# A second level of seven block products inside the gate/up stage of a two-layer kernel on one core

## The chip, the cores and the metric

The kernel runs on one core of a Trainium2 chip. The metric is the device time of one execution in microseconds (us), taken as the median of several executions. Ratios are the mean time of one kernel's runs over the mean of the kernel before's runs in the same rounds, so they are not quite the ratio of the medians quoted beside them.

Engine names as in the profile: PE is TensorE's matmuls, PEld its weight loads, DVE is VectorE, ACT is ScalarE, POOL is GpSimd, SP the engine that issues all DMA transfers here.

## The reference

Two layers, each a linear-attention block and a gated block, with 2048 tokens of width 1024 and an inner width of 3584:

```python
def _B_ref(x, w_gate, w_up, w_down):
    g = jnp.einsum("bsd,df->bsf", x, w_gate)
    u = jnp.einsum("bsd,df->bsf", x, w_up)
    h = g * u
    return jnp.einsum("bsf,fd->bsd", h, w_down)

x = A_x
x = x + _A_ref(_layernorm(x, axis=-1), A_wqkv, A_wo)
x = x + _B_ref(_layernorm(x, axis=-1), B_w_gate, B_w_up, B_w_down)
x = x + _A_ref(_layernorm(x, axis=-1), A_wqkv, A_wo)      # same weights again
x = x + _B_ref(_layernorm(x, axis=-1), B_w_gate, B_w_up, B_w_down)
```

Only the gated block B matters here: the gate and up products, and `h = g * u`.

## The kernel before

Block B handles 1024 tokens in a *pass*; there are two gate/up passes a layer, each followed by a down pass. I call the four gate/up passes 1a, 1b (layer one) and 2a, 2b (layer two).

Gate and up are already computed with Winograd's form of Strassen's scheme: the weight block and the token block are cut 2 x 2, and seven block products (numbered 1 to 7) replace eight. A *unit* is one such block multiplication for gate or for up. Each of its products is four matmuls with 512 columns:

```python
def pe(q, bank, start):
    w, rw, x, rx = xs[q]
    P.add("pe", lambda e: [e.matmul(psb(bank), w[:, k, :], x[:, k, :], start=(start and k == 0), stop=(k == 3),
                                    skip_group_check=True) for k in range(4)], rd=rw + rx, pwr=[bank])
```

The results that several products share are copied by ScalarE out of PSUM, the memory that matmuls write to, and added on VectorE while it evicts (moves a finished result out of PSUM, times the scale `SG`). VectorE also multiplies gate by up:

```python
def fin(b, bank, ti):          # b: which of four destination tiles
    ...
    elif m == 0:               # gate
        stt(g4[b], psb(bank), SG, tm[ti][0], tm[ti][1], gr, prd=[bank])
    else:                      # up: add, then multiply with gate
        ut, ur = utmp[b % 2], R(O_UT[b % 2], 1024)
        stt(ut, psb(bank), SG, tm[ti][0], tm[ti][1], ur, prd=[bank])
        tt(hv[:, j, :], ut, g4[b], ALU.mult, ur + gr, hr)
```

The sums of weight blocks for the first level are made on VectorE in pass 1a (`prep_s`), stored to DRAM and loaded in the other passes. In pass 1a VectorE also makes the sums for w_down and stores them from a tile `dout`:

```python
def wd_store(j):
    dma(tscr[:, :, j, :].rearrange("q p c -> p q c"), dout, R(V_D + j * 32, 32), KDW, rd=R(O_DOUT, 4096))
```

All tiles lie at hand-chosen byte offsets in one on-chip area, and every `P.add` lists the bytes it reads and writes; waits follow from these bytes. The relevant offsets of the kernel before:

```python
O_DOUT = RB + 28672                                  # 4096 bytes, to RB + 32768
O_UT = [RE + 4096 + i * 1024 for i in range(2)]      # utmp, two scratch tiles
```

Every transfer is issued by SP, in program order: weights come through a ring of five slots, one unit each, with `ring_issue()`.

## Time and profile before

1497.84 us median (1497.33 to 1498.81, 6 runs). From the page of the profile, the span, the busy time of each engine, and the chain of waits, which is the work that ended last, followed back:

```profile
span 1495.1 us, 17704 instructions
PE 1479.0 (99%) x6925; PEld 660.1 (44%) x6990; DVE 913.9 (61%) x1530; ACT 449.2 (30%) x732; POOL 216.0 (14%) x239
...
PE 91%; DVE 3%; DMA 3%; issue 1%; POOL 1%; ACT 1%; SPq 0%; ACTq 0%
```

The same busy times for the four gate/up passes alone, in the table of stretches. Columns: start and end in us, length, then busy us (and instructions) of PE, PEld, DVE, ACT and POOL, the granted clock, the DMA engines' busy share, GB/s. The lines are 1a, 1b, 2a, 2b.

```profile
243.15:412.86 169.71, 168.29 (x777) 72.12 (x777) 127.53 (x285) 66.11 (x113) 2.33 (x6) 1.00 0.83 254
498.98:666.68 167.70, 167.65 (x777) 72.19 (x777) 81.70 (x140) 65.53 (x112) 6.31 (x16) 1.00 0.73 210
983.68:1152.13 168.45, 167.83 (x777) 72.17 (x777) 72.74 (x122) 67.15 (x114) 2.36 (x6) 1.00 0.57 173
1238.25:1405.95 167.70, 167.65 (x778) 72.19 (x777) 67.08 (x108) 65.53 (x112) 0.00 (x0) 1.00 0.57 180
```

PE is busy for the whole of every pass. In the chain, in order of time (start, length, what), pass 1b is one piece:

```profile
499.14 167.49 PE ps L912 x776
```

So 776 matmuls in 167.49 us, 215.8 ns each, with nothing else in the way. Fewer or shorter matmuls save time here, for as long as the other engines and the transfers keep up. Note how much room they have: VectorE uses 40 to 49% of the last three passes, but 75% of pass 1a.

### The profile page before, as it was taken

The numbers are of one execution on the slowest core, as the hardware profiler recorded it, in microseconds if no ns is written. First come the engines' busy times: TensorE is split into PE (matmuls) and PEld (weight loads), VectorE is DVE, ScalarE is ACT, GpSimd is POOL, SyncE is SP. The second block draws the span as 40 slices with busy tenths as digits, with TensorE's granted clock in tenths as the row PEclk, the third lists the DMA queues.
The fourth block names the chain that finished last, engine by engine and source line by source line (L and its number), as shares of the span: only waits on it lengthen the run. The fifth ranks groups of instructions, "written<-read, shape, count | busy, mean of one in ns | idle before, by whom it ended". The sixth has DMA issues, their size and how long they took to land.

```text
span 1495.1 us, 17704 instructions
## 1 busy us (share of the span) xinstructions
PE 1479.0 (99%) x6925; PEld 660.1 (44%) x6990; DVE 913.9 (61%) x1530; ACT 449.2 (30%) x732; POOL 216.0 (14%) x239
## 2 busy tenths in 40 slices
PE   8999999999999999999999999999999999999999
PEld 4444444444444444444444444444444444444444
DVE  7986978777656463445488678764344553434453
ACT  3332355333300234330023314543333003334200
POOL 4544621000000010000044345310000000000000
PEclk9999999999999999999999999999999999999999
DMA  6134656799854896544466247555554455555352
GB/s 225 36 92 111 149 132 150 229 285 278 262 203 151 260 257 193 176 164 148 141 184 178 80 93 186 146 139 172 178 173 163 163 190 186 177 175 177 131 172 99
DMA packets 300643, 254.40 MB, mean 170 GB/s; under 512 B 102288, under 2 KB 266384, under 8 KB 300560
## 3 DMA queue, kind: packets, MB, share of 16 engines
q1 hardware_dynamic: 300560, 253.27, 57.4%
q8 instruction: 55, 0.90, 0.3%
q14 instruction: 28, 0.23, 0.0%
HBM read 195.04 MB, written 34.60 MB: 154 GB/s over the span
## 4 chain that ended last, share of the span: by engine, by line
PE 91%; DVE 3%; DMA 3%; issue 1%; POOL 1%; ACT 1%; SPq 0%; ACTq 0%
PE ps L912 43%; PE ps L1035 23%; PE ps L672 15%; PE ps L754 7%; PE ps L840 2%; DMA arena<-in_B_w_down_dram 1%; DVE arena L610 1%; DVE arena L412 1%; DMA arena<-arena 1%; DMA arena<-in_A_wqkv_dram 1%; POOL arena L701 1%; PE ps L766 0%; PE ps L794 0%; SPq L386 0%; POOL arena L417 0%
## 5 line engine op out<-in xcount | busy, mean ns | idle before, releaser
L912 PE MATMUL ps<-arena 128*128 128x512 f16 x3136 | 679.0, 379 | 1.9 <-DVE arena L613 1.3
L613 DVE SCALAR_TENSOR_TENSOR arena<-ps,arena 128x512 f16<-128x512 f32 (+2 forms) x480 | 327.2, 689 | 470.6 <-PE ps L912 161.8
L912 PEld LDWEIGHTS ps<-arena 128*128 128x128 f16 (+1 forms) x3136 | 291.4, 98 | 388.2 <-ACT arena L916 36.0
L1035 PE MATMUL ps<-arena 128*128 128x512 f16 (+1 forms) x1548 | 338.0, 379 | 1.1
L1035 PEld LDWEIGHTS ps<-arena 128*128 128x128 f16 x1568 | 153.5, 98 | 185.0
L672 PE MATMUL ps<-arena 128*128 128x512 bf16 x1003 | 222.1, 379 | 4.6 <-DMA arena<-in_A_wqkv_dram 1.6
L916 ACT ACTIVATE arena<-ps 128x512 f32<-128x512 f32 x224 | 133.7, 597 | 291.1 <-PE ps L912 288.9
L610 DVE TENSOR_TENSOR arena<-arena 128x512 f16<-128x512 f16 (+3 forms) x360 | 197.9, 574 | 18.3 <-DMA arena<-in_B_w_down_dram 8.3
L672 PEld LDWEIGHTS ps<-arena 128*128 128x128 f16 x1024 | 99.6, 98 | 122.4 <-DMA arena<-in_A_wqkv_dram 2.1
L558 ACT ACTIVATE arena<-ps 128x512 f32<-128x512 f32 x128 | 76.4, 597 | 232.6 <-PE ps L672 218.4
L938 ACT COPY ps<-ps 128x512 f32<-128x512 f32 x112 | 63.9, 570 | 204.3 <-PE ps L912 203.7
L754 PE MATMUL ps<-arena 128*128 128x512 bf16 x500 | 114.6, 379 | 0.6
L840 PE MATMUL ps<-arena 128*128 128x512 bf16 x502 | 110.8, 379 | 3.2 <-ACT ps L834 2.7
L415 POOL TENSOR_SCALAR arena<-arena 128x1 f32<-128x1 f32 x64 | 20.7, 323 | 598.7 <-DVE arena L414 598.7
L412 DVE BATCH_NORM_STATS2 arena<-arena 128x6 f32<-128x512 bf16 x128 | 88.1, 689 | 13.1 <-DMA arena<-in_A_x_dram 6.7
L701 POOL TENSOR_TENSOR arena<-arena 128x1024 f16<-128x1024 f32 x32 | 79.8, 2493 | 90.3 <-DVE arena L699 83.7
L926 ACT ACTIVATE arena<-ps 128x512 f16<-128x512 f32 x112 | 66.9, 597 | 84.5 <-PE ps L912 84.5
L561 DVE SCALAR_TENSOR_TENSOR arena<-ps,arena 128x512 bf16<-128x512 f32 x128 | 88.5, 692 | 4.4
L684 POOL TENSOR_TENSOR arena<-arena 128x512 f32<-128x512 f32 x60 | 74.6, 1248 | 87.0 <-DVE arena L561 85.6
L559 DVE TENSOR_SCALAR arena<-arena 128x512 f32<-128x512 f32 x128 | 65.9, 515 | 27.7 <-ACT arena L558 26.6
L840 PEld LDWEIGHTS ps<-arena 128*128 128x128 f16 x512 | 49.8, 98 | 63.9 <-ACT ps L834 4.4
L754 PEld LDWEIGHTS ps<-arena 128*128 128x128 f16 x512 | 49.3, 98 | 55.7
(45 smaller groups left out, 381.9 us busy)
## 6 DMA issues: line engine op xcount, KB each, us to landing
arena<-s_scratch SPq DMA_DIRECT2D x84, 512.0 KB, 3.3
arena<-in_B_w_gate_dram SPq DMA_DIRECT2D x56, 512.0 KB, 4.2
arena<-in_B_w_up_dram SPq DMA_DIRECT2D x56, 512.0 KB, 3.9
arena<-t_scratch SPq DMA_DIRECT2D x32, 896.0 KB, 4.8
arena<-in_B_w_down_dram SPq DMA_DIRECT2D x24, 896.0 KB, 4.6
s_scratch<-arena SPq DMA_DIRECT2D x28, 512.0 KB, 6.9
arena<-in_A_wqkv_dram SPq DMA_DIRECT2D x12, 1024.0 KB, 8.3
arena<-in_A_x_dram SPq DMA_DIRECT2D x31, 256.0 KB, 3.2
```

The source lines that it names most:

```text
L412: P.add("dve", (lambda h: lambda e: e.bn_stats(st[j][:, 6 * h:6 * h + 6], x_res[:, i, (D // 2) * h:(D // 2) * (h + 1)]))(h), rd=r_x(i, (D ...
L558: P.add("act", lambda e: e.activation(etmp[r], psb(bank), AF.Exp), prd=[bank], wr=er)
L561: P.add("dve", lambda e: e.scalar_tensor_tensor(out=dst_ap, in0=psb(bank), scalar=0.0, in1=etmp[r], op0=ALU.max, op1=ALU.add), prd=[bank], ...
L610: P.add("dve", lambda e: e.tensor_tensor(out=out, in0=a, in1=b, op=op), rd=rd, wr=wr, prd=prd)
L613: P.add("dve", lambda e: e.scalar_tensor_tensor(out=out, in0=a, scalar=sc, in1=b, op0=ALU.mult, op1=op1), rd=rd, wr=wr, prd=prd)
L672: return [e.matmul(psb(bank), xnT[:, k, i * 128:(i + 1) * 128], w[:, k, h * 512:(h + 1) * 512], start=(k == 0), stop=(k == KT - 1)) for k ...
L701: P.add("pool", lambda e: e.tensor_tensor(out=asb[b].rearrange("p (h c) -> p h c", c=32), in0=pbuf.rearrange("p (h c) -> p h c", c=32), in ...
L754: return [e.matmul(psb(bank), xr[:, t, j * 128:(j + 1) * 128], pk[:, h, t, :], start=(t == 0), stop=(t == NST - 1)) for t in range(NST)]
L840: return [e.matmul(psb(bank), xnT[:, g, i * 128:(i + 1) * 128], wp[:, g, dh * 512:(dh + 1) * 512], start=(dh == 0 and g == 0), stop=(g == ...
L912: P.add("pe", lambda e: [e.matmul(psb(bank), w[:, k, :], x[:, k, :], start=(start and k == 0), stop=(k == 3), skip_group_check=True) for k ...
L916: P.add("act", lambda e: e.activation(tm[i][0], psb(bank), AF.Copy, scale=SG), prd=[bank], wr=tm[i][1])
L1035: return [e.matmul(psb(bank), hv[:, 7 * hf + k, t * 128:(t + 1) * 128], w[:, k, :], start=(start and hf == 0 and k == 0), stop=(hf == 1 an ...
```

## The change

The intent: apply the seven-product scheme once more, inside some of the products. For a *pair* of units (A: gate, B: up, same output columns) the product q of both is a multiplication of a 2 x 2 weight block [wA; wB] with a 2 x 2 token block. Written as seven products again, 2 x 4 matmuls of 512 columns become 7 x 2 of 256. It is done for products 2 and 4 in pass 1b and for 2, 3 and 4 in passes 2a and 2b; 1a keeps one level. With 14 pairs a pass that is 112 pair-products. The joins run on VectorE and ScalarE. The new weight sums are made on VectorE in 1b, stored to DRAM and loaded in 2a and 2b.

```diff
-    SG = 16.0
+    SG = 4.0
+    L2SETS = {(False, 0): "", (False, 1): "24", (True, 0): "234", (True, 1): "234"}
+    ORDER0 = "P1A P5A P6A D2A P7A D3B' R0 P1B D4A T0 P6B D3A P7B P5B T1 R1 D4B D2B"
+    ORDER1 = "T0 21 P1A P1B 26 P6A 41 D3B' 27 P6B S3= D2A 46 P7A D2B P7B P5A 47 R D4A D4B S2+ P5B D3A T1"
+    ORDER2 = "P1A 21 P1B D3A' 26 P6A 27 T0 D2A D3B' S3= D2B 41 P6B 46 P7A 31 47 P7B D4A 36 D4B P5A P5B R S2+ T1 37"
 ...
-    O_G4 = RE
-    O_UT = [RE + 4096 + i * 1024 for i in range(2)]
+    O_UT = [RE + 6144, RB + 31744]
+    O_TP = {"3": RE, "2": RE + 3072, "4": RB + 28672}
 ...
+        def sp_place(ps_, p, q):
+            sz, so = (2048, 0) if q == "2" else (1024, 2048)
+            return sz, so, O_X + (8 * ps_ + 6) * D * 2 if q == "2" else O_R + 12288, R(V_SP + 64 * p + so // 64, 32)
 ...
+                    def mm(i, bank, half, start):
+                        (w, rw), (xx, rxx) = qs[i]
+                        P.add("pe", lambda e: [e.matmul(psb(bank)[:, 256 * half:256 * half + 256], w[:, k, :], xx[:, k, :], ...)
+                                               for k in range(2)], rd=rw + rxx, pwr=[bank])
 ...
+                    def st6():
+                        mm(5, yk, 0, True)
+                        acp(c5, rc5, yk)                 # ScalarE, 256 columns
+                        mm(6, xk, 0, False)
+                        acp(ss[:, 1], rss[1], xk)
+                        tt(ss[:, 1], ss[:, 1], c5, ALU.add, rss[1] + rc5, rss[1])
 ...
+                def sums(q, mode):
+                    if mode == "load":
+                        sp_load(ps_, p, q)
+                        return
 ...
+                    tt(sp[:, 0], wB[:, 0:2], wB[:, 2:4], ALU.add, rB, rp[0])
+                    tt(sp[:, 1], sp[:, 0], wA[:, 0:2], ALU.subtract, rp[0] + rA, rp[1])
+                    tt(sp[:, 2], wA[:, 0:2], wB[:, 0:2], ALU.subtract, rA + rB, rp[2])
+                    tt(sp[:, 3], wA[:, 2:4], sp[:, 1], ALU.subtract, rp[1] + rA, rp[3])
+                    dma(spscr[p, :, so:so + sz], vh(o, sz), rv, KSPW[q], rd=R(o, 2 * sz))
```

The order strings are read so: `P6A` is first-level product 6 of unit A; `26` is step 6 of the second level of product 2; `D2A` finishes destination 2 of unit A; `R` issues two ring loads; `S3=` makes (1b) or loads (2a, 2b) this pair's sums for product 3, and `S2+` the next pair's for products 2 and 4; `T` runs pending other work, such as layer-norm; `'` means the pair before.

## The prediction

> **What bounds the kernel now.** TensorE. The page gives PE 1479.0 of 1495.1 us busy, at full granted clock in all 40 slices, and the chain of waits is 91% PE, 43% of it in the gate/up line. In the table of stretches each of the four gate/up passes (784 matmuls of 128x512) lasts about 169 us with PE busy throughout: 776 matmuls run in 167.49 us in one unbroken piece of the chain, 215.8 ns each. In the last two VectorE is busy 71 and 68 us, ScalarE 66.
>
> **What the change does.** In the second pass of layer one, two of the seven products, and in both passes of layer two, three, are split once more: for a pair of units 8 matmuls of 512 columns become 14 of 256. Pairs times products: 14 x (2+3+3) = 112. The instruction order shows 1568 new 256-wide matmuls and 896 fewer 512-wide. First pass: same products, new order.
>
> **TensorE saving.** The trace has no 256-wide matmul. Groups of four 128-wide ones with different weights take 0.23 us (start to next start), 57 ns each. The Trainium skill ("TensorE: Matmul & The Clock Gate", Back-to-back issue gap) gives N/2.4 + 2.5 ns, which fits both traced sizes; my estimate for 256 is 109 ns. 14 x 109 = 1.53 us against 8 x 0.216 = 1.73: 0.2 us per pair and product, 22 us in all. All of it is critical while PE stays fed: floor about 1476 us.
>
> **What it adds.** VectorE: 84 more evictions from PSUM (688 ns alone, about 0.60 back to back), 280 two-input operations of 256 elements (most f32), 220 of 512 (most f16). For f32 two-input the Trainium skill ("VectorE: DVE Perf Modes", perf-mode tier table) says 1x; I estimate 0.42 us (256) and 0.69 (512), less back to back. ScalarE: 448 copies of 128x256 (about 0.38 us by estimate) for 84 full ones. Per pair of units, by estimate:
> - layer two: PE 11.5 us, VectorE 10 to 10.5, ScalarE 8. Loaded, but PE still leads; some 0.2 us per pair lost on copies between steps of one chain (about 3 us a pass), plus 1 to 2 us at the start, where twelve new block differences precede the first chain.
> - layer one, second pass: PE 11.7 us, VectorE 10 to 11 (it also makes the weight sums for later), plus about 16 us of layer-norm over the pass. VectorE is on the edge, so most of the 5.5 us gain is eaten: 166 to 172 us against 169.
> DMA: 0.75 MB more per pair, prefetched; not bound.
>
> **Sum.** Layer-two passes 162 to 164 each (-11 in all), layer one's second pass about -2, first pass 0 to +1, start of layer two +1: about -14 us. Predicted 1484 us, range 1476 to 1495. The saving cannot reach 2% (30 us): faster 0.02, same 0.96, slower 0.02.
>
> **What would show each step.** 256-wide starts 109 ns apart; PE busy throughout both layer-two passes, each 5 to 8 us shorter; VectorE near 90% busy there and above 90% in layer one's second pass, where weight loads wait for VectorE or ScalarE copies and PE has gaps; down passes unchanged, about 84 us.
>
> **What would make it wrong.** VectorE saturated in layer two too (dependent pairs don't overlap): passes near 169, time near 1495. 256-wide matmuls above 123 ns would erase the gain (8 x 216/14). Or the new order of the first pass stalls on the just-in-time weight sums.

## The result, and the profile after

1497.32 us median (1493.72 to 1497.9, 6 runs). The ratio to the kernel before is 0.9992, with a 95% interval of 0.9979 to 1.0005: no change. It lies outside the predicted range.

The page of the changed kernel:

```profile
span 1496.2 us, 20408 instructions
PE 1465.1 (98%) x7597; PEld 730.5 (49%) x7662; DVE 1152.0 (77%) x2122; ACT 538.7 (36%) x1096; POOL 217.1 (15%) x239
...
PE 75%; DVE 11%; DMA 10%; issue 2%; POOL 1%; ACT 1%; SPq 1%; DVEq 0%; ACTq 0%
```

In the lines of this kernel's traces L967 are first-level and L1040 second-level matmuls, L634 two-input operations and L637 evictions on VectorE, L1044 ScalarE's copies within the second level; in the edited kernels the numbers are up to seven higher.

PE works 14 us less, VectorE 238 us more, and the chain of waits, 91% PE before, now has 21% VectorE and DMA in it. The table of stretches for 1a, 1b, 2a, 2b:

```profile
242.81:418.56 175.75, 170.07 (x781) 70.97 (x781) 129.12 (x290) 66.89 (x114) 2.37 (x6) 1.00 0.87 264
503.82:675.83 172.01, 166.81 (x950) 90.90 (x950) 158.06 (x364) 83.95 (x196) 6.78 (x16) 1.00 0.84 259
992.51:1158.07 165.56, 162.22 (x1032) 99.01 (x1032) 149.08 (x294) 103.20 (x254) 2.85 (x6) 1.00 0.76 234
1243.15:1408.07 164.92, 161.42 (x1031) 99.38 (x1031) 141.06 (x272) 101.70 (x252) 0.00 (x0) 1.00 0.75 241
```

Passes 2a and 2b became shorter, 1a and 1b longer. The basic saving is real: in the timeline of PE (start, length of the group, what) two second-level steps of four matmuls start 0.44 us before what follows them, 109 ns a matmul:

```profile
1272.84 0.60 PE L1040 MATMUL ps<-arena 128*128 128x256 f16 x4
1273.28 1.03 PE L967 MATMUL ps<-arena 128*128 128x512 f16 x4
```

Since four of the eight matmuls that ran after the start of each down pass now run before it, I count each gate/up pass together with its down pass, from the first matmul of the one to the first of the next stage. "Matmuls alone" is 0.198 us (8 x 215.8 ns less 14 x 109.2 ns) for each of the 14 pairs and each split product.

| gate/up and down pass | before | after | difference | matmuls alone | lost |
|---|---|---|---|---|---|
| 1a | 255.83 | 261.01 | +5.2 | 0 | 5.2 |
| 1b | 253.82 | 257.26 | +3.4 | -5.5 | 8.9 |
| 2a | 254.57 | 250.64 | -3.9 | -8.3 | 4.4 |
| 2b | 256.85 | 253.05 | -3.8 | -8.3 | 4.5 |

The rest of the program differs by 0.2 us in all. So 22 us were saved and 23 us lost in the same four places. The next section asks what each loss is.

**Pass 1a** makes the same products as before. The list of waits for it (who waited for whom: us in total, times, longest) has one large line of which the kernel before has nothing, and the timelines of VectorE and PE show one of these waits and a gap of PE behind an eviction:

```profile
DVE arena L637 <- DMA t_scratch<-arena: 20.1, 11, 3.9
```

```profile
317.35 0.69 DVE L637 SCALAR_TENSOR_TENSOR arena<-ps,arena 128x512 f16<-128x512 f32 x1 [2.73 <-DMA t_scratch<-arena]
...
322.41 3.63 PE L967 MATMUL ps<-arena 128*128 128x512 f16 x16 [1.26 <-DVE arena L637]
```

An eviction by VectorE waits for a *store* of w_down's sums. It does not use those sums. But the change moved the second scratch tile `utmp[1]` to RB + 31744, the last KB of `dout` (RB + 28672 to RB + 32768), from which that store reads. So the eviction into this tile, which comes before the multiply of each unit B, has to wait until the store has read it.

**Pass 1b**, in the chain of waits, in order of time (SPq is SP issuing a transfer); with a period of 12.76 us from one issue of the w_up load to the next (562.78 less 550.02), where the matmuls of a pair need 11.7 (40 x 215.8 ns and 28 x 109.2 ns):

```profile
548.94 0.71 DVE arena L634 x3
...
549.66 0.32 SPq L396
...
550.02 4.48 DMA arena<-in_B_w_up_dram
...
554.52 0.44 DVE arena L634
...
561.69 0.71 DVE arena L634 x3
...
562.42 0.32 SPq L396
...
562.78 4.44 DMA arena<-in_B_w_up_dram
```

VectorE makes the sums of product 3 (548.94), SP stores them (549.66) and only then issues the load of the next pair's up weights (550.02), which stands behind that store in program order. VectorE needs these weights for the next pair's sums (554.52), then works through the evictions of a pair, and the loop closes. PE is not in it. After 613 us, when the layer-norm work of this pass has run out, the chain is PE alone.

**Passes 2a and 2b** have waits of PE for the loaded sums. The lines of the two lists of waits, 2a first, and one such wait in the timeline of 2b:

```profile
PE ps L1040 <- DMA arena<-sp_scratch: 1.8, 4, 0.7
...
PE ps L1040 <- DMA arena<-sp_scratch: 2.9, 5, 1.2
...
1281.28 0.60 PE L1040 MATMUL ps<-arena 128*128 128x256 f16 x4 [0.26 <-DMA arena<-sp_scratch]
```

The buffer for the sums of products 2 and 4 is single: the load can start only after the last reader of the pair (`D4A`) and must land before step `26` of the next pair, some 5 us later by my count of the matmuls between them. The list of DMA issues for 2b gives 4.5 us from issue to landing, so there is hardly any margin:

```profile
arena<-sp_scratch SPq DMA_DIRECT2D x13, 512.0 KB, 4.5
```

### The profile page after: what moved, and what is told of

It is laid out like the page before. It is cut to its first block, busy times and chain, and to the rows that moved or that the text cites. A ratio compares the mean times of both kernels' runs of the same rounds, so it can differ in the third digit from the quotient of the medians.

```text
span 1496.2 us, 20408 instructions
## 1 busy us (share of the span) xinstructions
PE 1465.1 (98%) x7597; PEld 730.5 (49%) x7662; DVE 1152.0 (77%) x2122; ACT 538.7 (36%) x1096; POOL 217.1 (15%) x239
## 4 chain that ended last, share of the span: by engine, by line
PE 75%; DVE 11%; DMA 10%; issue 2%; POOL 1%; ACT 1%; SPq 1%; DVEq 0%; ACTq 0%
PE ps L1225 23%; PE ps L967 19%; PE ps L716 15%; PE ps L1040 8%; PE ps L798 7%; DVE arena L634 5%; DMA arena<-sp_scratch 3%; DVE arena L637 2%; DMA arena<-in_B_w_up_dram 2%; DVE arena L422 2%; DMA t_scratch<-arena 2%; PE ps L884 2%; DMA arena<-arena 1%; DMA sp_scratch<-arena 1%; SPq L396 1%
## 5 line engine op out<-in xcount | busy, mean ns | idle before, releaser
L967 PE MATMUL ps<-arena 128*128 128x512 f16 x2240 | 535.5, 379 | 10.2 <-DVE arena L637 3.7
L637 DVE SCALAR_TENSOR_TENSOR arena<-ps,arena 128x512 f16<-128x512 f32 (+2 forms) x564 | 377.4, 686 | 200.7 <-PE ps L1225 144.5
L634 DVE TENSOR_TENSOR arena<-arena 128x512 f16<-128x512 f16 (+6 forms) x868 | 404.7, 493 | 50.5 <-ACT arena L1044 27.2
L967 PEld LDWEIGHTS ps<-arena 128*128 128x128 f16 (+1 forms) x2240 | 212.0, 98 | 225.5 <-ACT arena L972 19.2
L1225 PEld LDWEIGHTS ps<-arena 128*128 128x128 f16 x1568 | 153.5, 98 | 184.1
L1040 PE MATMUL ps<-arena 128*128 128x256 f16 x1568 | 221.8, 273 | 7.3 <-DMA arena<-sp_scratch 4.7
L1040 PEld LDWEIGHTS ps<-arena 128*128 128x128 f16 (+1 forms) x1568 | 149.7, 98 | 94.2 <-ACT arena L1044 13.5
L1044 ACT ACTIVATE arena<-ps 128x256 f32<-128x256 f32 x448 | 155.3, 384 | 110.7 <-PE ps L1040 107.0
L716 PEld LDWEIGHTS ps<-arena 128*128 128x128 f16 x1024 | 100.0, 98 | 122.0 <-issue 1.6
```

What stands on the lines that cost most here:

```text
L634: P.add("dve", lambda e: e.tensor_tensor(out=out, in0=a, in1=b, op=op), rd=rd, wr=wr, prd=prd)
L637: P.add("dve", lambda e: e.scalar_tensor_tensor(out=out, in0=a, scalar=sc, in1=b, op0=ALU.mult, op1=op1), rd=rd, wr=wr, prd=prd)
L716: return [e.matmul(psb(bank), xnT[:, k, i * 128:(i + 1) * 128], w[:, k, h * 512:(h + 1) * 512], start=(k == 0), stop=(k == KT - 1)) for k ...
L1040: P.add("pe", lambda e: [e.matmul(psb(bank)[:, 256 * half:256 * half + 256], w[:, k, :], xx[:, k, :], start=(start and k == 0), stop=(k == ...
L1044: P.add("act", lambda e: e.activation(dst, psb(bank)[:, 0:256], AF.Copy, scale=SG), prd=[bank], wr=rd_)
L1225: return [e.matmul(psb(bank), hv[:, 7 * hf + k, t * 128:(t + 1) * 128], w[:, k, :], start=(start and hf == 0 and k == 0), stop=(hf == 1 an ...
```

## The experiments

All use the changed kernel as base. The kernel before ran on the same chip in the same rounds each time: 1496.85 us for the first four, 1496.79 for the next three, 1496.58 for the next three, 1496.72 for the last.

One caution on the lengths of single passes: in six of the profiles (`e5_spread` to `e10_no_store`) the first matmul of each down pass is recorded, in the others its record is missing (six matmuls stand there for seven weight loads). A pass without its down pass therefore reads 0.2 us shorter in these six. Differences between the two groups are given with the down pass, which this does not touch.

### Pass 1a: the scratch tile

```diff
-    O_UT = [RE + 6144, RB + 31744]
+    O_UT = [RE + 6144, RB + 31744, RE + 4096]
 ...
-                        ut, ur = utmp[c], R(O_UT[c], 1024)
+                        cu = 2 if c == 1 and first and ps_ == 0 else c
+                        ut, ur = utmp[cu], R(O_UT[cu], 1024)
```

> One edit to the changed kernel: in layer one's first gate/up pass the second scratch tile of the multiply on VectorE moves out of the area from which the w_down sums are stored to DRAM. Theory (false sharing: that multiply waits for the store, 2.7 us at a time, and VectorE behind it): first pass 175.8 us falls to 169 to 171, VectorE's waits for the t_scratch store vanish, total about 5 us below the changed kernel, 1492. Rival (new order of the products bunches VectorE's work in this pass): the pass stays above 174 us and PE still waits for VectorE.

Measured: 1493.72 us, ratio 0.9977 (0.9965 to 0.9990), by medians 3.6 us below the changed kernel where about 5 was expected. Pass 1a takes 170.46 us, with its down pass 255.72, as before the change (255.83). No wait for the t_scratch store is left in the list of waits of this pass. The new order of the products costs nothing; the whole loss of 1a was the shared KB.

### Pass 1b: the place of the ring loads

```diff
-    ORDER1 = "... 41 D3B' 27 P6B S3= D2A 46 P7A D2B P7B P5A 47 R D4A D4B S2+ ..."
+    ORDER1 = "... 41 D3B' R 27 P6B S3= D2A 46 P7A D2B P7B P5A 47 D4A D4B S2+ ..."
```

> One edit to the changed kernel: in layer one's second pass the two ring loads per pair are issued before the store of the third product's weight sums instead of after it; all engines' work is unchanged. Theory (a loop: sums on VectorE, store queued on SP, w_up load queued behind that store, next sums waiting for the load; 12.75 us a pair in the first 8 pairs): the pass falls from 172.0 to 164 to 168 us, total 4 to 8 us lower. Rival, my prediction's reason (VectorE saturated by its own work): the pass stays within 1.5 us of 172.0, as VectorE's work is the same.

Measured: 1492.19 us, ratio 0.9969 (0.9956 to 0.9981). Pass 1b falls by 3.7 us to 168.29 (without this edit it took 171.65 to 172.76 us in three profiles). That is 0.3 us above the range of the loop theory, and clearly out of what the rival allowed. With its down pass it takes 253.54, about as before the change (253.82), so the 5.5 us that the matmuls save were still missing. The chain of waits from 548 to 575 us now holds VectorE and nothing else but issue time, where before the w_up load stood in it for 4.48 us of every 12.76. Whether that means that VectorE was full had to be tested separately (below).

### Pass 2b: two buffers for the sums

```diff
+            o2 = O_XN[0] if not RG["first"] and ps_ == 1 and p % 2 else O_X + (8 * ps_ + 6) * D * 2
-            return sz, so, O_X + (8 * ps_ + 6) * D * 2 if q == "2" else O_R + 12288, R(...)
+            return sz, so, o2 if q == "2" else O_R + 12288, R(...)
```

> One edit to the changed kernel: in layer two's last pass the 512 KB sums of products two and four have two buffers in turn, so their load can start a pair earlier. Theory (PE waits for a load that can only start when the last reader is done, some pairs 11.9 to 12.8 instead of 11.5 us): the last pass falls from 164.9 to 161 to 162.5 us, the pass before stays at 165.6; total 2 to 4 us lower. Rival (ScalarE copies between steps of a chain cost those 4 us): last pass stays above 164 us.

Measured: 1495.55 us, ratio 0.9992 (0.9979 to 1.0004): no gain to be seen. Pass 2b took 163.87 us here; in the three profiles with one buffer it took 164.92, 163.38 and 164.08. A miss for the theory as I had put it, and not a proof of the rival.

### The three edits together

> The three edits together. If the three causes are separate they add up: 11 to 16 us below the changed kernel, 1481 to 1487 us, 0.988 to 0.993 of the kernel before. If one bottleneck stands behind all of them, clearly less than the sum of the three single gains.

Measured: 1487.31 us (1487.0 to 1490.2, 5 runs), ratio 0.9939 (0.9926 to 0.9953). By medians that is 10 us below the changed kernel, short of the 11 to 16 that I expected. By ratios (0.9992 for the changed kernel) the single gains are 2.2, 3.4 and 0 us, each known to 2 to 3 us, and together they give 7.9. Within that, the three together earn no less than the sum of what they earn one by one, and there is no sign of one bottleneck behind all of them. In the profile of this run 1a takes 170.32 and 1b 168.05 us, as in the single edits.

### A null edit

```diff
-                if u % 4 < 2 and not is_last and nxt.t_next < 8:
+                if u % 2 == 0 and not is_last and nxt.t_next < 8:
```

> On top of the three edits: in layer one's second pass the layer-norm steps of the next layer run one a pair over the whole pass instead of two in every other pair (same work in all). Theory (what is left there, 168 us against 163 of pure matmul time, is VectorE being full in the first pairs): the pass falls by 1.5 to 4 us, to 164 to 166.5. Rival (the pass is held by loads and stores, its DMA share is 0.8 to 0.9): no change beyond 1 us.

Measured: 1488.69 us, ratio 0.9946 (0.9933 to 0.9958); pass 1b with its down pass 252.91 us against 253.30. This tells nothing, because the edit hardly changes anything: `T1` is the last token of a pair and `T0` the first of the next, so the steps were already one pair apart. I had not looked at the order of the tokens. The run is useful for one thing: pass 2b, whose code is the same as with the three edits, took 166.40 us here and 163.16 there. How long PE waits for the sums varies between executions.

### Layer two without the loads

```diff
         def sp_load(ps_, p, q):
+            if p > 0:
+                return
 ...
-    SG = 4.0
+    SG = 1.0
```

> On top of the three edits, wrong result on purpose: in both passes of layer two only the first pair's sums are loaded, the other pairs use what lies in the buffers (the scale constant is 1 instead of 4, so that the wrong numbers stay finite; it costs no time). Theory (the 3 to 4 us that these passes still lose are waits for these loads and the traffic they add): both passes fall to 161 to 162 us, total 4 to 6 us below the version with three edits. Rival (ScalarE copies between the steps of one chain): passes stay at 163 to 165 us.

Measured: 1482.49 us, ratio 0.9903 (0.9889 to 0.9916), wrong result. 2a takes 162.37 us, a little above the 161 to 162 expected, and 2b 161.67. With their down passes that is 247.66 us (250.48 with the three edits) and 249.99 (251.13 to 254.72 in four profiles with two buffers). So the loads, their waits and their traffic together, did cost 2.8 us in 2a and 1.1 to 4.7 in 2b, and the ScalarE copies between the steps of a chain cost next to nothing: the list of waits for 2a, without the loads, still shows weight loads waiting for the copies as often as before, but PE itself idles 0.8 us for them in the whole pass (in this kernel L1044 is the second-level matmuls and L1048 the copies):

```profile
PEld ps L1044 <- ACT arena L1048: 5.8, 29, 0.8
...
PE ps L1044 <- ACT arena L1048: 0.8, 2, 0.5
```

### Pass 1b without the second level

```diff
-    L2SETS = {(False, 0): "", (False, 1): "24", ...
+    L2SETS = {(False, 0): "", (False, 1): "", ...
```

> On top of the three edits, layer one's second pass without the second level (its matmuls all 512 wide again), while it still makes and stores the weight sums that layer two loads. If the second level earns nothing there because VectorE gives back what TensorE saves: this pass with its down pass stays within 1 us (253.3 us now, 253.8 in the kernel before). If it does earn: up to 5 us longer.

Measured: 1489.93 us, ratio 0.9957 (0.9944 to 0.9971). 1b with its down pass takes 255.24 us, 1.3 to 1.9 more than with the second level (253.30 to 253.92 in three profiles). So it earns 1.3 to 1.9 us of 5.5 there. My bound for "earns nothing" was 1 us, so the answer lies between the two.

### Pass 2b: the place of the load in SP's queue

```diff
+    ORDER3 = ORDER2.replace("R S2+ T1", "S2+ R T1")      # for pass 2b only
```

> On top of the three edits: in the last pass the load of the next pair's sums (now with two buffers) is queued on SP before the four ring loads of the pair, not after them. Theory (the second buffer earned nothing because the earlier load only stood behind the ring loads: it landed 8.2 us after its issue, 4.5 with one buffer): it lands in 5 us or less, PE stops waiting for it, the last pass falls from 163 to 166 (four profiles with two buffers) to 161 to 162, total 1 to 4 us lower. Rival (the traffic as such is too much): no change.

Measured: 1484.78 us (1484.62 to 1485.53, 4 runs), ratio 0.9918 (0.9903 to 0.9933). 2b takes 160.92 us. The list of DMA issues in 2b (size, us to landing), first with the three edits, then with this one:

```profile
arena<-sp_scratch SPq DMA_DIRECT2D x13, 512.0 KB, 8.2
```

```profile
arena<-sp_scratch SPq DMA_DIRECT2D x13, 512.0 KB, 4.1
```

This is why the second buffer alone earned nothing. With one buffer the load waited on SP for its reader and then took 4.5 us. With two it could be issued a pair earlier, but right behind four ring loads of 512 KB, and landed after 8.2 us (8.4 in the run with the second buffer alone). In front of them it lands in 4.1 us and nobody waits for it. The Trainium skill ("DMA: Bandwidth & Descriptors", Two DMAs through the same engine are not ordered) says that, within one queue of one DMA engine, descriptors start in order; these two lines agree with that. The list of waits of PE for 2b is down to one wait of 0.5 us at the first pair, and 2b with its down pass takes 249.27 us, 7.6 below the kernel before, of 8.3 that the matmuls alone would give.

### Pass 1b: VectorE or the DMA engines

In 1b, even with the ring loads moved, both VectorE (39.07 of 40 us busy from 540 to 580) and the DMA engines (0.95) are full. Two runs tell them apart. The first leaves VectorE work out and keeps all transfers, the second does the opposite.

```diff
                     tt(sp[:, 0], wB[:, 0:2], wB[:, 2:4], ALU.add, rB, rp[0])
+                    if q == "2" or p == 0:
                     tt(sp[:, 1], ...); tt(sp[:, 2], ...); tt(sp[:, 3], ...)
```

> On top of that, wrong result on purpose: in layer one's second pass three of the four VectorE operations that make the third product's sums are left out for all pairs but the first (39 operations, 9 to 11 us of VectorE); loads and stores stay. Theory (VectorE is full in the first two thirds of the pass): the pass falls from 168 to 164 to 166 us. Rival (the DMA engines, 0.96 busy there, hold it): within 1 us of 168.

Measured: 1481.42 us, ratio 0.9894 (0.9879 to 0.9909). 1b falls from 168.44 to 163.80 us, and its chain is 99% PE. (The comparison with the reference passed within its tolerance, although three quarters of these sums are wrong by construction; that it passes does not show that all sums are right, here or in any other run.)

```diff
-                    dma(spscr[p, :, so:so + sz], vh(o, sz), rv, KSPW[q], rd=R(o, 2 * sz))
+                    if p == 0:
+                        dma(spscr[p, :, so:so + sz], vh(o, sz), rv, KSPW[q], rd=R(o, 2 * sz))
```

> The counterpart, wrong result on purpose: VectorE makes all sums, but they are stored for the first pair only (and not loaded later, as without the loads experiment before). If VectorE holds layer one's second pass, it stays within 1 us of 168; if the DMA engines hold it, it falls by 2 us or more. Both passes of layer two at 161 to 162.5 again.

Measured: 1483.33 us, ratio 0.9908 (0.9891 to 0.9924), wrong result. 1b stays at 167.64 us though the DMA share from 540 to 580 falls to 0.75; 2a takes 162.37 and 2b 160.93 us. The table of stretches from 540 to 580, with all work (the edited order), with VectorE work left out, with stores left out:

```profile
540.00:580.00 40.00, 39.04 (x225) 21.23 (x223) 39.07 (x91) 18.79 (x46) 3.40 (x8) 1.00 0.95 274
```

```profile
540.00:580.00 40.00, 40.00 (x236) 22.93 (x235) 39.20 (x87) 20.57 (x48) 3.27 (x8) 1.00 0.97 292
```

```profile
540.00:580.00 40.00, 38.73 (x222) 20.93 (x220) 39.06 (x92) 18.79 (x47) 3.39 (x8) 1.00 0.75 213
```

Read the first number after the length, PE's busy time, and the count of matmuls in brackets behind it: only less VectorE work lets more matmuls through (236 against 225 and 222). VectorE holds this pass, not the DMA engines at 0.97.

### A version that beats both

VectorE has room in pass 1a, where it is busy 128 of 170 us. So the sums of product 3 are made and stored there, and no longer in 1b:

```diff
-    ORDER0 = "P1A P5A P6A D2A P7A D3B' R0 P1B ..."
+    ORDER0 = "P1A P5A P6A D2A P7A D3B' R0 S3= P1B ..."
-    ORDER1 = "... 27 P6B S3= D2A 46 ..."
+    ORDER1 = "... 27 P6B D2A 46 ..."
 ...
+                    if ps_ == 0:
+                        o = O_X + 4 * D * 2          # free in pass 1a
```

> A version meant to beat both kernels, results right: the four edits, and the third product's weight sums are made and stored in layer one's first pass, where VectorE is busy 128 of 170 us, instead of in the second, where it is full. If VectorE's load is what holds the second pass: it falls from 168.4 to 164 to 165.5 us and the first pass stays within 1.5 us of 170.2 (its DMA share is 0.87, so it may not stay); total 1480 to 1483 us. Rival: the first pass pays as much as the second gains, total 1484 to 1487.

Measured: 1483.39 us (1483.03 to 1485.07, 5 runs), ratio 0.9912 (0.9899 to 0.9926), comparison with the reference passed. The median is 0.4 us above the expected range. With the down passes, 1b falls by 4.9 us (253.92 to 248.97), as expected of VectorE; 1a rises by 1.9 (255.68 to 257.53), a little more than I allowed, and 2a was 1.3 us longer in this profile. Against the version without this step (1484.78 us, 0.9918) the intervals of the ratios overlap, so only the step from the kernel before is sure: 0.9% faster.

## Why the prediction was wrong

What held:

- *256-wide starts 109 ns apart.* Measured 0.44 us for four. The formula from the Trainium skill ("TensorE: Matmul & The Clock Gate", Back-to-back issue gap) fitted, and the saving of 22 us of matmul time is there: with the obstacles removed, 2b becomes 7.6 us shorter of the 8.3 to be had, 2a without its loads 6.9 of 8.3, 1b 4.9 of 5.5 in the last version (248.97 us against 253.82 with its down pass).
- *VectorE and ScalarE loads.* 256-wide f32 adds took 419 ns (0.42 estimated), the ScalarE copies 384 ns (0.38). VectorE was 90% busy in 2a, 86% in 2b and 92% in 1b (158.06 of 172.01 us), as predicted.
- *The saving cannot reach 2%.* It could not, in any version.

The mechanism of the saving was right. What failed is the step that took the transfers and the moved tiles to cost nothing: loads that were to be "prefetched" stood in SP's queue behind stores, readers and other loads, and a moved scratch tile had to wait for a store. Term by term of the sum:

- *"first pass 0 to +1"*: +5.2 us. This is the largest miss for which the reading had no warning at all. I compared products and instruction counts, which are the same in 1a, and did not lay the new byte offsets over the old ones. The listed risk, a stall on the just-in-time weight sums, was not it: the stall was an eviction waiting for an unrelated store, because a scratch tile had been moved into the tile that is being stored. Moving it out brought 1a back to 255.72 us with its down pass.
- *"layer one's second pass about -2"* (166 to 172 us): 172.0 us for the pass, +3.4 with its down pass, so the last us of the range. The reason, VectorE on the edge, was half of it. One half was a loop through SP's queue, 3.7 us when undone; the other half was VectorE's own work, 4.6 us when a part of it was left out.
- *"DMA: 0.75 MB more per pair, prefetched; not bound."* This step failed twice. The next pair's weights were issued behind a store that waits for VectorE (1b), and the sums have one buffer, so their load cannot start before the last reader is done (2a, 2b). By bytes there was room: the DMA engines were 0.75 to 0.76 busy in layer two. What mattered was when a transfer could be issued and what stood before it.
- *"Layer-two passes 162 to 164 each (-11 in all)"*: 165.6 and 164.9 us, -7.7 in all. The 3 us a pass that I had set down for ScalarE copies between steps were not lost to these; they hardly stop PE. About as much was lost to the loads of the sums: 2.8 us in 2a, gone when the loads were left out, and 3.8 us in 2b (253.05 to 249.27 with its down pass), gone when the load had a second buffer and came first in the queue. What is left in 2a without the loads is 1.4 us by the table (6.9 of 8.3), of which the list of waits shows 0.8 us for ScalarE and 0.4 us for VectorE at the start of the pass. The further +1 that I had set down for the start of layer two does not show: outside the four places of the table the two kernels differ by 0.2 us.

What stays open: 2a has no second buffer in any version, since no room for it was found; that its 3 us would go the way of 2b's was not tried, and neither was the new place in the queue with the one buffer. The 1.9 us that 1a paid in the last version have the look of VectorE (140 of 172 us busy) or DMA (0.92 busy), but were not taken apart. Why the waits in 2b varied by 3 us between executions of the same code is not known either.

## What to carry to other kernels

When a change removes work from the engine that bounds a kernel, look in the order of the other queues for what now closes a loop: a store that waits for an engine delays every load behind it (3.7 us in 1b), and a second buffer is worth little if its load is queued behind four others (8.2 us to landing against 4.1). When a change moves tiles by hand, lay the old and the new byte ranges over each other and look for a reader that is a DMA; such a collision costs time in a stage that the change does not seem to touch. And read a gain that "does not show" by stage: here 22 us were saved and 23 lost in the same run, and a single total would have told neither.

## What the Trainium skill lacked or had wrong

- "TensorE: Matmul & The Clock Gate", Back-to-back issue gap: for streams of weight load and matmul it gives a sustained 81 ns at 128 columns and 131 ns at 512, and calls N/2.4 + 2.5 the gap of an isolated matmul. In these traces streams with a weight load for every matmul ran at 56 to 57 ns (128 columns), 109 ns (256) and 215.8 ns (512): the formula holds for the stream, and the two sustained figures do not.
- "VectorE: DVE Perf Modes", The DRAIN you can't avoid: it says that a next operation that is not held starts earlier than after the flush of the one ahead, and gives no figure for how much earlier. Nine two-input operations of 512 f16 elements took 3.36 us in a row in pass 1a, where one alone takes 0.42: (3.36 - 0.42) / 8 is 0.37 us from start to start. An operation that needs the result before it gains nothing: in the kernel before, a multiply starts 0.73 us after the start of the 0.69 us eviction that feeds it. So summing single durations overstates what VectorE needs for independent operations.
- "VectorE: DVE Perf Modes", the errata section's cycle table: ScalarE from PSUM to on-chip memory at 172 + N cycles gives 357 ns for 256 columns and 570 for 512, by estimate; the traces show 384 and 597 ns, 27 ns more in both.
- "DMA: Bandwidth & Descriptors": it has the order of descriptors in one queue, but no page gives a number for what it costs a load to be queued behind others. Here the same 512 KB landed after 4.1 us ahead of four loads of 512 KB and after 8.2 us behind them.
